# Four pieces of weight decoding move from slots 3 and 4 to slots 20 to 23

## The chip, the cores and the metric

The kernel runs on one core of a Trainium2 chip. The metric is the device time of one execution in microseconds (us), lower is better. Engines: PE is TensorE (matrix products), DVE is VectorE, ACT is ScalarE, POOL is GpSimd, and SP is SyncE, whose queue issues the DMA transfers.

## What is computed

Three stages follow each other. A recurrent state of 40x40 per batch and head walks over 768 steps and gives one vector per step; the 3072 vectors go through a first MLP (320 to 1024, a softmax-gated unit, a layer norm, back to 320) and a second one (320 to 2048, a leaky unit, back to 320). Cut to what matters:

```python
for t in range(S):                                   # S = 768, 4 batches x 8 heads, D = 40
    y[:, :, t] = np.einsum('bhd,bhde->bhe', rt, state)
    Sa = np.einsum('bhde,bhe->bhd', state, at)
    state_decay = state * wt[:, :, None, :] - np.einsum('bhd,bhe->bhde', Sa, bt)
    state = state_decay + np.einsum('bhd,bhe->bhde', vt, kt)
...
h = x @ w_in                                         # first MLP, 3072 x 320 -> 1024
e = np.exp(h - h_max)
solu = h * e / (np.sum(e, axis=-1, keepdims=True) + 1e-09)
ln = (solu - mu) / np.sqrt(var + 1e-06) * g_ln
x = ln @ w_out                                       # 1024 -> 320
...
h = x @ w_in                                         # second MLP, 320 -> 2048
g = np.maximum(h, 0.0) + alpha * np.minimum(h, 0.0)
out = g @ w_out                                      # 2048 -> 320
```

## The kernel before

**Slots.** The recurrence is cut into 24 slots of 32 steps (`slot(g)`, g from 0 to 23). In each slot the state enters as `px` (L430, copied to `XP` by ACT at L433; this document counts a slot from that copy), then `pu` = `XP` times an inverted triangular matrix `LMN` (L443), `pf` (L466), `pst` and the state update `VUS` (L478, L483), `pss` (L501), `py` (L541), and so to the next slot's `px`. Every fourth slot needs a new inverse: its elimination steps (L355 and L359 alternately, some 30 pairs of shrinking or growing width) run on DVE through two slots and end in a transposition, L388; the first `pu` that reads it is that of slot 4, 8, 12 and so on. Scans over the decay (L281, L277) and factors for the key tiles (`kbf`, L303) are DVE's too; `kbf` is loaded by L230, two transfers per two slots.

**The first MLP lags.** In slot g the tokens of step group g-3 go through the first product (`mm1`, L576, from `xt` to `h`) and the softmax (`soft`: L581 row maximum on DVE, L582 exponential on ACT, L583 on DVE, L585 square on ACT, which frees `h`); those of group g-4 are normed (L593), transposed (`tr1`, L615, to `lnh` at L620 and `lnl` at L621) and go through the second product (`mm2`, L629 to L631). `mm1` of the next group needs `h` free. PE's order is written out by hand and is the same in both kernels, instruction for instruction. The other engines are put in order by a scheduler when the program is built, so the change moves rows on them that the diff doesn't show.

**Weight decoding.** The weights arrive in 64-bit floats and are turned to 32 bits on the chip in 51 pieces (11 for the first MLP, 40 for the second). `dec(n)` in `slot` takes the next n pieces off one list, always in the same order. A piece loads `raw` (L681, SP), runs `decode`: L657 and L658 on DVE, L659 and L660 on ACT, L661 and L663 on DVE, L666 on POOL; a piece of the second MLP is then written to DRAM (L717, SP; to `wd` or `od`). The first pieces are 512 wide, the later ones 256. A 256-wide piece has buffers of its own. A **wide** piece borrows the MLP's: `raw` takes the buffer of `lnh` or `P` (alternating) and `wem` that of `lnl`, each of which exists once. Piece 16 (counted from 0) is the last wide one; its `raw` sits in `P`, the buffer that `soft` writes, and is both read and overwritten there, so that `P` is free only when its L717 has left.

**Phase 2.** After slot 23 the second MLP runs; its weights come back from `wd` and `od` through `w2l` (L964, L965), split by ACT (L966) and POOL (L968, L969).

How many pieces a slot takes is set by tables: `ND` for slots 0 to 3, `NL` for slots 20 to 23, `NC` for the others, by g % 4.

## Time and profile before

| | |
|---|---|
| median of 3 runs | 1150.07 us (1148.67 to 1155.81) |
| the profiled execution | 1149.97 us, its span 1148.2 us |
| busy, PE / DVE / ACT / POOL | 976.5 / 790.7 / 519.9 / 496.7 us |
| mean granted clock of PE | 0.896 of full speed |
| slots 3, 4 | 176.2 to 206.6 to 247.4 us |
| slots 6, 7, 8 | 275.7 to 302.8 to 324.6 to 362.5 us |
| slots 20 to 23 | 667.0 to 695.3 to 720.3 to 739.7 us and on |
| second MLP alone | from about 818 us to the end |

No engine is busy all the time in phase 1: the slots are chains that pass from engine to engine. So the question at each place is which wait ends last there. A row of the timeline gives the start, the time, the engine, the line, the operation and in brackets how long the engine stood idle before and who released it.

### The profile page before, as it was taken

To read this page: it belongs to the slowest core of one execution; us is meant where nothing else is said; L and a number is where in the kernel's file an instruction comes from. 1 tells how busy PE (TensorE), PEld (TensorE's weight loads), DVE (VectorE), ACT (ScalarE), POOL (GpSimd) and SP (SyncE) were. 2 spreads that over 40 slices of the span, in tenths; PEclk is the share of its full clock that TensorE was granted. 3 is DMA by queue.
4 is the path that set the end of the run, shared out by engine and by line. 5 is a ranking of instruction groups with operands and counts; after the bars stand their busy time and mean duration, and the time that the engine had idled before them with its cause. 6 is when DMAs were issued, how large, how long until landed. Compare 5 with 4: busy or idle time off the path is not lost.

```text
span 1148.2 us, 37076 instructions
## 1 busy us (share of the span) xinstructions
PE 976.5 (85%) x15913; PEld 810.8 (71%) x15934; DVE 790.7 (69%) x1610; ACT 519.9 (45%) x1198; POOL 496.7 (43%) x546
## 2 busy tenths in 40 slices
PE   6275686688888988798888887989999999999997
PEld 3243454476666767677667666778999988888897
DVE  8899689877997898888978966467444444444433
ACT  3435454376547663765466647656312121212121
POOL 6847454444444443443344425345333333333332
PEclk8687878699888888986888889999999999999999
DMA  5513335344434433442334333354202020201000
GB/s 166 149 49 92 97 113 145 94 110 110 116 104 104 118 94 95 109 128 73 102 94 105 102 111 98 100 169 134 91 1 69 1 69 1 69 1 47 1 23 15
DMA packets 104543, 99.52 MB, mean 87 GB/s; under 512 B 38068, under 2 KB 83764, under 8 KB 104372
## 3 DMA queue, kind: packets, MB, share of 16 engines
q1 hardware_dynamic: 104372, 97.07, 30.5%
q8 instruction: 127, 2.08, 0.8%
q14 instruction: 44, 0.36, 0.1%
HBM read 71.62 MB, written 25.43 MB: 85 GB/s over the span
## 4 chain that ended last, share of the span: by engine, by line
PE 49%; DVE 29%; ACT 6%; issue 6%; POOL 5%; DMA 4%; SPq 0%; DVEq 0%; POOLq 0%; ACTq 0%
PE ph L1016 15%; PE h L576 5%; PE acc L1036 5%; PE acc L1035 5%; PE acc L1034 5%; DVE LMN L359 4%; DVE tmp L355 3%; DMA kbf<-in_kb_fm_dram 3%; DVE VUS L483 2%; DVE H L277 2%; PE pf L466 2%; DVE KBS L509 2%; DVE XS L336 2%; DVE kbf L303 1%; PE pg L326 1%
## 5 line engine op out<-in xcount | busy, mean ns | idle before, releaser
L1023 POOL TENSOR_TENSOR gll<-gt,gh 128x512 fp32r<-128x512 f32 (+1 forms) x112 | 129.0, 1152 | 224.0 <-ACT gh L1022 222.9
L596 DVE TENSOR_SCALAR gt<-ph,al 128x512 f32<-128x512 f32 (+1 forms) x112 | 75.5, 674 | 189.7 <-PE ph L1016 189.6
L1022 ACT CAST gh<-gt 128x512 fp32r<-128x512 f32 (+1 forms) x112 | 62.5, 559 | 254.5 <-DVE gt L597 212.6
L576 PE MATMUL h<-w1h,xt 128*128 128x512 f32 x240 | 106.4, 492 | 15.7 <-ACT h L585 15.7
L312 POOL TENSOR_TENSOR XS<-XS,H 40x512 f32<-40x512 f32 (+1 forms) x48 | 68.5, 1432 | 87.2 <-DVE H L277 50.6
L1035 PE MATMUL acc<-w2l,gh 128*128 128x320 f32 x288 | 89.0, 309 | 0.0
L1034 PE MATMUL acc<-w2h,gh 128*128 128x320 f32 x288 | 89.0, 309 | 0.0
L1036 PE MATMUL acc<-w2h,gll 128*128 128x320 f32 x288 | 88.9, 309 | 0.0
L529 POOL TENSOR_TENSOR YS<-YS,mask 64x512 f32<-64x512 f32 x48 | 64.2, 1337 | 49.0 <-ACT YS L528 44.4
L211 PE MATMUL busy<-busy 128*128 128x512 bf16 x200 | 60.1, 454 | 24.6 <-DVE tmp L355 19.6
L359 DVE TENSOR_TENSOR LMN<-LMN,tmp 128x87 f32<-128x87 f32 (+25 forms) x189 | 75.9, 413 | 2.7
L355 DVE TENSOR_TENSOR tmp<-LMN,LMN 128x87 f32<-128x87 f32 (+25 forms) x189 | 71.9, 392 | 3.4
L597 DVE SCALAR_TENSOR_TENSOR gt<-ph,gt 128x512 f32<-128x512 f32 (+1 forms) x112 | 68.8, 615 | 3.7
L576 PEld LDWEIGHTS h<-w1h,xt 128*128 128x128 f32 x240 | 51.2, 224 | 25.5 <-ACT h L585 17.8
L576 PE MATMUL h<-w1l,xt 128*128 128x512 f32 x144 | 68.8, 478 | 0.0
L629 PE MATMUL po<-wo1h,lnh 128*128 128x320 f32 x192 | 66.9, 348 | 0.5 <-DVE lnl L621 0.5
L630 PE MATMUL po<-wo1l,lnh 128*128 128x320 f32 x192 | 61.5, 320 | 0.0
L631 PE MATMUL po<-wo1h,lnl 128*128 128x320 f32 x192 | 61.5, 320 | 0.0
L1016 PE MATMUL ph<-w1h,w2h 128*128 128x512 f32 x180 | 59.3, 394 | 0.0
L211 PEld LDWEIGHTS <-busy 128*128 128x128 bf16 x221 | 23.0, 112 | 50.9 <-DVE busy L946 19.3
L326 PE MATMUL pg<-XS,kbf 104*32 104x64 f32 x1536 | 39.6, 243 | 21.6 <-DVE kbf L303 10.8
L582 ACT ACTIVATE P<-h,sm 128x1024 f32<-128x1024 f32 x24 | 26.7, 1114 | 63.0 <-DVE sm L581 60.5
(200 smaller groups left out, 2738.6 us busy)
## 6 DMA issues: line engine op xcount, KB each, us to landing
kbf<-in_kb_fm_dram SPq DMA_DIRECT2D x24, 416.0 KB
x2d<-x SPq DMA_DIRECT2D x24, 320.0 KB
xd<-Y SPq DMA_DIRECT2D x24, 256.0 KB
xt<-xd SPq DMA_DIRECT2D x12, 512.0 KB
raw<-in_w_in_dram SPq DMA_DIRECT2D x20, 256.0 KB
wt<-in_w_fm_dram SPq DMA_DIRECT2D x24, 211.7 KB
raw<-in_w_in_dram SPq DMA_DIRECT2D x8, 512.0 KB
raw<-in_w_out_dram SPq DMA_DIRECT2D x16, 256.0 KB
```

The source lines that it names most:

```text
L211: nc.tensor.matmul(st["busy"], lhsT=busy[:, 0:128], rhs=busy, start=True, stop=True)
L312: (nc.vector if w < 2 and e in DA else nc.gpsimd).tensor_tensor(out=o, in0=o, in1=h, op=ALU.mult)
L355: eng.tensor_tensor(out=tv[:, a - rows[0][0]:b - rows[0][0]], in0=M[:, a:b, s:s + 1].to_broadcast(sh), in1=l.unsqueeze(1).to_broadcast(sh) ...
L359: r = eng.tensor_tensor(out=o, in0=o, in1=tv[:, a - rows[0][0]:b - rows[0][0]], op=ALU.add)
L576: nc.tensor.matmul(st["h"][:, ns], lhsT=l, rhs=r, start=j == 0, stop=j == len(ops) - 1)
L596: nc.vector.tensor_scalar(out=tmp, in0=h, scalar1=0.0, scalar2=al, op0=ALU.min, op1=ALU.mult)
L597: nc.vector.scalar_tensor_tensor(out=o, in0=h, scalar=0.0, in1=tmp, op0=ALU.max, op1=ALU.add)
L1016: nc.tensor.matmul(p, lhsT=l, rhs=r, start=j == 0, stop=j == len(ops) - 1)
L1023: nc.gpsimd.tensor_tensor(out=gll, in0=t, in1=f32(gh), op=ALU.subtract)
L1034: nc.tensor.matmul(acc, lhsT=gh[:, cs], rhs=oh, start=f == 0, stop=False)
L1035: nc.tensor.matmul(acc, lhsT=gh[:, cs], rhs=ol, start=False, stop=False)
L1036: nc.tensor.matmul(acc, lhsT=gll[:, cs], rhs=oh, start=False, stop=f == K2 - 1)
```

## The change

The tables move four pieces. Pieces per slot before: 6, 6, 4, 2 in slots 0 to 3, then 2, 3, 1, 0 four times, then 3, 3, 3, 0. After: 6, 6, 4, 0, then 0, 3, 1, 0, then 2, 3, 1, 0 three times, then 4, 4, 4, 1. The order of the pieces stays, so from slot 3 on every slot works on pieces up to four places further back in the list: piece 16, the wide one, is called in slot 5 in place of slot 3.

```diff
-VS, NC, NL = 0, (2, 3, 1, 0), (3, 3, 3, 0)
-ND = (6, 6, 4, 2)
+VS, NC, NL = 0, (2, 3, 1, 0), (4, 4, 4, 1)
+ND = (6, 6, 4, 0)
...
         nd = (ND if g < 4 else NL if g >= NG - 4 else NC)[g % 4]
+        if g == KEND:
+            nd = 0
         invs(0.2)
```

`KEND` is 4. Lines below this place are two higher in the changed kernel (L964 to L969 become L966 to L971).

**DVE in slot 3, the last third of the inverse that slot 4 uses.** L355 and L359 are the elimination steps; `sm` holds the softmax's columns of token group 0. Before, the softmax's L583 stands behind the inverse's end:

```order
L355 TENSOR_TENSOR tmp<-LMN_162,LMN_160 128x87
L359 TENSOR_TENSOR LMN_162<-LMN_162,tmp 128x29x3
L384 SCALAR_TENSOR_TENSOR LMN_162<-LMN_162,LMN_160 128x30 x2
L384 SCALAR_TENSOR_TENSOR LMN_162<-LMN_162,LMN_160 128x31
L388 STREAM_TRANSPOSE LMN_160<-LMN_162 128x32x32
L583 SCALAR_TENSOR_TENSOR P,sm<-h,P 128x1024
L586 TENSOR_SCALAR sm<-sm 128x1
L657 TENSOR_SCALAR em_2620<-raw_2619 128x256
L584 TENSOR_SCALAR sm<-sm 128x1
L587 TENSOR_SCALAR sm<-sm 128x1
```

In the changed kernel it stands earlier, between elimination steps of width 231 and 220; the four operations on `wem` of the wide piece, which stood before the step of width 192, are gone from here:

```order
L359 TENSOR_TENSOR LMN_162<-LMN_162,tmp 128x20x12
L483 TENSOR_TENSOR VUS_163<-pst,VUS_164 40x320
L355 TENSOR_TENSOR tmp<-LMN_162,LMN_160 128x231
L583 SCALAR_TENSOR_TENSOR P,sm<-h,P 128x1024
L359 TENSOR_TENSOR LMN_162<-LMN_162,tmp 128x21x11
L584 TENSOR_SCALAR sm<-sm 128x1
L586 TENSOR_SCALAR sm<-sm 128x1
L355 TENSOR_TENSOR tmp<-LMN_162,LMN_160 128x220
L587 TENSOR_SCALAR sm<-sm 128x1
```

L583 moved from behind L388 to some 25 rows ahead of it; L582 on ACT moves with it, to right behind L528 of the same slot.

**DVE in slot 6, the first half of the inverse that slot 8 uses.** `lnl` is the buffer of the second product's low half, `ptr` the transposed tokens. Before, the two L621 of token group 2 stand at the start of the inverse:

```order
L367 STREAM_TRANSPOSE LMN_162<-LMN_161 128x32x32
L621 TENSOR_TENSOR lnl<-ptr,lnh 128x512
L483 TENSOR_TENSOR VUS_164<-pst,VUS_163 40x320
L384 SCALAR_TENSOR_TENSOR LMN_161<-LMN_162,LMN_161 128x31
L384 SCALAR_TENSOR_TENSOR LMN_161<-LMN_162,LMN_161 128x30 x2
L483 TENSOR_TENSOR VUS_164<-pst,VUS_163 40x320
L355 TENSOR_TENSOR tmp<-LMN_161,LMN_162 128x87
L483 TENSOR_TENSOR VUS_164<-pst,VUS_163 40x320
L359 TENSOR_TENSOR LMN_161<-LMN_161,tmp 128x3x29
L483 TENSOR_TENSOR VUS_164<-pst,VUS_163 40x320
L355 TENSOR_TENSOR tmp<-LMN_161,LMN_162 128x112
L621 TENSOR_TENSOR lnl<-ptr,lnh 128x512
```

In the changed kernel the wide piece comes first, behind the row maximum L581 of the next token group, and L621 follows it:

```order
L581 TENSOR_REDUCE sm<-h 128x1
L657 TENSOR_SCALAR wem<-raw 128x512
L658 TENSOR_SCALAR wem<-raw 128x512
L359 TENSOR_TENSOR LMN_161<-LMN_161,tmp 128x10x22
L355 TENSOR_TENSOR tmp<-LMN_161,LMN_162 128x231
L661 SCALAR_TENSOR_TENSOR wem<-raw,wem 128x512
L663 SCALAR_TENSOR_TENSOR wem<-raw,wem 128x512
L359 TENSOR_TENSOR LMN_161<-LMN_161,tmp 128x11x21
L355 TENSOR_TENSOR tmp<-LMN_161,LMN_162 128x240
L621 TENSOR_TENSOR lnl<-ptr,lnh 128x512 x2
L359 TENSOR_TENSOR LMN_161<-LMN_161,tmp 128x12x20
L355 TENSOR_TENSOR tmp<-LMN_161,LMN_162 128x247
```

The two L621, one at the inverse's first rows and one after its second pair of steps before, now stand together behind step 240, behind the wide piece's `wem`, which holds the `lnl` buffer until its L666 on POOL has read it. Two rows further on moved with them: L545, which waits for `py` and stood ahead of the inverse's first step of width 220, now stands some fourteen steps later, behind the second one of width 255; and in slot 7 the softmax's L583, which stood 22 rows ahead of L388, now stands five rows behind it.

**SP where phase 1 ends, in slot 23 and just behind.** `od_103<-dec` writes decoded pieces, `xd<-Y` and `xt<-xd` move the recurrence's last outputs to the first MLP, `w2l` are the decoded weights that come back. Before:

```order
L717 DMA od_103<-dec 128x256
L965 DMA w2l_11902<-od_101 128x640
L560 DMA xd_79<-Y 32x8x256
L560 DMA xd_79<-Y 8x8x256
L560 DMA xd_79<-Y 32x8x256
L560 DMA xd_79<-Y 8x8x256
L561 DMA xt<-xd_79 128x4x256
L650 DMA x2d_89<-x_11937 640x1x128
L562 DMA xt<-xd_79 128x256
```

In the changed kernel:

```order
L717 DMA od_103<-dec 128x256
L681 DMA raw_11540<-in_w_out_dram 128x512
L560 DMA xd_79<-Y 32x8x256
L560 DMA xd_79<-Y 8x8x256
L717 DMA od_103<-dec 128x256
L681 DMA raw_11751<-in_w_out_dram 128x512
L560 DMA xd_79<-Y 32x8x256
L560 DMA xd_79<-Y 8x8x256
L717 DMA od_103<-dec 128x256
L561 DMA xt<-xd_79 128x4x256
L562 DMA xt<-xd_79 128x256
```

Before, one decoded piece is still to be written here, ahead of the last moves of `Y`; now three are, each behind its own chain of decoding, and two loads of `raw` stand between, all ahead of the `xt` loads.

## Rows read from the trace of the kernel before

**Rows 1.** Page, part 4: the chain that ended last, shares of the span by engine

```profile
PE 49%; DVE 29%; ACT 6%; issue 6%; POOL 5%; DMA 4%; SPq 0%; DVEq 0%; POOLq 0%; ACTq 0%
```

**Rows 2.** Stretches: start:end and length, busy us (x instructions) per engine, clock, DMA

```profile
206.60:247.40 40.80, 26.43 (x644) 21.17 (x645) 35.26 (x75) 23.11 (x52) 17.14 (x19) 0.79 0.36 92
695.30:777.00 81.70, 72.51 (x1439) 61.72 (x1438) 47.30 (x104) 52.03 (x112) 34.24 (x38) 0.98 0.43 125
818.00:1148.20 330.20, 322.43 (x1845) 293.07 (x1843) 131.38 (x198) 66.78 (x123) 115.98 (x98) 0.99 0.10 28
```

**Rows 3.** DVE in slots 3 and 4: start, us, line, operation, [idle before, releaser]

```profile
193.31 1.21 DVE L581 TENSOR_REDUCE sm<-h 128x1 f32<-128x1024 f32 x1
...
199.68 0.42 DVE L657 TENSOR_SCALAR wem<-raw 128x512 int32<-128x512 int32 x1
...
201.63 0.68 DVE L663 SCALAR_TENSOR_TENSOR wem<-raw,wem 128x512 f32<-128x512 uint32 x1
...
206.67 1.30 DVE L355 TENSOR_TENSOR tmp<-LMN,LMN 128x156 f32<-128x156 f32 x1
208.01 0.32 DVE L359 TENSOR_TENSOR LMN<-LMN,tmp 128x156 f32<-128x156 f32 x1
...
212.01 2.01 DVE L388 STREAM_TRANSPOSE LMN<-LMN 128x1024 f32<-128x1024 f32 x1
```

**Rows 4.** ACT in slot 4

```profile
210.03 1.11 ACT L582 ACTIVATE P<-h,sm 128x1024 f32<-128x1024 f32 x1 [2.46 <-DMA od<-raw]
```

**Rows 5.** POOL in slot 4

```profile
206.53 1.26 POOL L666 TENSOR_TENSOR raw<-wem 128x512 f32<-128x512 f32 x1
```

**Rows 6.** SP (the DMA queue's issues) in slots 4 and 5

```profile
207.82 0.35 SPq L717 DMA_DIRECT2D od<-raw  x1
...
251.76 0.63 SPq L650 DMA_DIRECT2D x2d<-x  x1
254.10 0.36 SPq L717 DMA_DIRECT2D wd<-dec  x1
254.83 0.33 SPq L230 DMA_DIRECT2D kbf<-in_kb_fm_dram  x1
```

**Rows 7.** PE in slot 4

```profile
217.10 0.79 PE L576 MATMUL h<-w1h,xt 128*128 128x512 f32 x1 [10.63 <-ACT h L585]
...
221.73 0.39 PE L576 MATMUL h<-w1l,xt 128*128 128x512 f32 x1
222.05 0.79 PE L443 MATMUL pu<-XP,LMN 32*32 32x40 f32 x64
```

**Rows 8.** Chain of waits, first transfers of wide pieces: start, us, what

```profile
155.80 4.06 DMA raw<-in_w_in_dram
```

**Rows 9.** DVE in slot 6

```profile
283.66 0.69 DVE L621 TENSOR_TENSOR lnl<-ptr,lnh 128x512 fp32r<-128x512 f32 x1
...
294.68 1.21 DVE L581 TENSOR_REDUCE sm<-h 128x1 f32<-128x1024 f32 x1
```

**Rows 10.** PE in slots 6 to 8

```profile
285.39 0.38 PE L615 MATMUL ptr<-ident,P 128*128 128x128 f32 x2
...
288.67 0.31 PE L629 MATMUL po<-wo1h,lnh 128*128 128x320 f32 x1
...
297.63 0.80 PE L430 MATMUL px<-VUS,XS 104*32 104x40 f32 x64 [2.45 <-DVE Yt L545]
...
304.99 1.29 PE L443 MATMUL pu<-XP,LMN 32*32 32x40 f32 x64
...
329.47 0.78 PE L443 MATMUL pu<-XP,LMN 32*32 32x40 f32 x64 [4.02 <-DVE LMN L388]
```

**Rows 11.** Groups by line and shape: DVE work of 256-wide pieces (count, busy, mean ns)

```profile
L658 DVE TENSOR_SCALAR em<-raw 128x256 int32<-128x256 int32 x36 | 18.0, 500 | 0.0
...
L663 DVE SCALAR_TENSOR_TENSOR em<-raw,em 128x256 f32<-128x256 uint32 x36 | 17.3, 480 | 0.4 <-ACT em L660 0.3
L657 DVE TENSOR_SCALAR em<-raw 128x256 int32<-128x256 int32 x36 | 16.8, 466 | 5.3 <-DMA raw<-in_w_in_dram 2.6 <-DMA raw<-in_w_out_dram 1.7 <-POOL Y L550 0.7
...
L661 DVE SCALAR_TENSOR_TENSOR em<-raw,em 128x256 int32<-128x256 int32 x36 | 16.2, 450 | 5.6 <-ACT em L659 4.8
```

**Rows 12.** DVE in slot 20

```profile
709.46 1.80 DVE L663 SCALAR_TENSOR_TENSOR em<-raw,em 128x256 f32<-128x256 uint32 x1
```

**Rows 13.** SP where phase 1 ends

```profile
763.74 0.38 SPq L561 DMA_DIRECT2D xt<-xd  x1
```

**Rows 14.** PE where phase 1 ends

```profile
777.75 0.48 PE L576 MATMUL h<-w1h,xt 128*128 128x512 f32 x1
```

## Prediction

> **What bounds the kernel now.** I read the page's chain first: PE holds 49% of it, DVE 29% [rows 1]. Then I cut the span into stretches. From about 818 us on, only the second MLP runs: PE is busy 322.43 of 330.20 us [rows 2]. The change touches nothing there but the last loads of its weights, so this stretch is fixed and the time is decided in the slots before it. There, DVE is the fullest engine in slot 4 (35.26 of 40.80 us) but far from full in slots 21 to 23 and just behind (47.30 of 81.70 us) [rows 2]. So decoding costs more in slot 4 than at the end, if DVE's busy time alone decided. The timelines say that waits decide as much, and where they sit.
>
> **The wait that the change removes (slots 3 and 4).** The row maximum of token group 0 ends on DVE at 194.52 [rows 3]. The exponential that needs it starts only at 210.03, and its releaser is the transfer `od<-raw` [rows 4]: the wide piece sits in buffer `P` from its load to its store. Its DVE work runs from 199.68 to 202.31 [rows 3], POOL multiplies from 206.53 to 207.79 [rows 5], SP issues the store at 207.82 [rows 6], and 2.2 us later `P` is free. Behind it wait L583, L585, then `mm1` on PE, which stood idle for 10.63 us until 217.10, and behind `mm1`, in PE's fixed order, `pu` of slot 4 at 222.05 [rows 7]. In the changed kernel L582 and L583 are in slot 3, before the inverse's last third, so `h` is free before `px(4)`, and `mm1` runs in PE's idle time. What `pu` then waits for is the inverse: L388 ends at 214.02 [rows 3]. DVE loses there the wide piece's four operations and gains L583, about even, since DVE waits for `py` in between anyway. One step of 128x156 took 1.30 us beside POOL's L666, against 0.32 us for its neighbour of the same width [rows 3, 5]; without the wide piece that is 0.98 us less. So L388 ends at about 213.0 and `pu` moves from 222.05 to 213.0: **9.0 us earlier at this point**.
>
> How much is left at the start of slot 6? DVE has only 40.80 - 35.26 = 5.54 us of idle time in slot 4 [rows 2], so a PE that runs ahead soon waits for DVE. But pieces 18 and 19 leave slot 4 too. A 256-wide piece costs DVE 500 + 480 + 466 + 450 ns = 1.90 us [rows 11]. Two are 3.80 us, and 5.54 + 3.80 = 9.34 us would allow the 9.0. In slot 5 the second `kbf` load is issued at 254.83, behind the store of a decoded piece at 254.10, and the chain of slot 5 goes through it; the store of the first MLP's output, at 251.76 for 0.63 us, is the next one in front [rows 6]. Without the decoded piece the load goes out at 252.39 less the shift of the slot itself. Bounds for the gain at slot 6: 3.8 us, if only the DVE work counts, and 9.0 us, if all of `pu`'s shift lives on. I take **8.0**, near the upper end, because DVE, `pu` and the load all move by about this much.
>
> **The wait that it makes (slots 6 to 8).** Piece 16 now runs in slot 6. Its `raw` needs `P`, which the transposition of token group 2 reads until PE's L615 at 285.39 [rows 10]; a wide load then takes some 4.06 us [rows 8], so it lands at 290 at the earliest. But its DVE rows stand behind L581, at 294.68 to 295.89 [rows 9]. The four of them took 2.63 us in slot 3 [rows 3], so they end at about 298.5; L666 takes 1.26 us [rows 5], 299.8; then both L621, 0.69 us each [rows 9]: the first product that reads `lnl` can start at about 300.5 to 301. Before, L621 ran at 283.66 [rows 9] and `mm2` of group 2 began at 288.67 [rows 10]. PE thus waits about 12 us in times of the kernel before, with `py` and `px(7)` queued behind. `px(7)` stood at 297.63, with 2.45 us of waiting for DVE [rows 10]; it comes some 9 to 11.5 us later, and `pu(7)`, at 304.99, about 9.3 us later. After that there is slack: DVE goes on with the inverse for slot 8 in the meantime, and before the change PE waited 4.02 us for L388 at `pu(8)`, 329.47 [rows 10]. 9.3 - 4.0 = 5.3. The inverse itself loses almost nothing, as more of its steps now stand ahead of L545, which waits for `py`. But L583 of the next token group now stands behind L388 in DVE's order, so the `mm1` that waits for it in slot 7 can't run ahead of the inverse's end. I take a **loss of 5.0 us**; bounds 1.0 (the inverse alone decides `pu(8)`) and 11.5 (all of `px(7)`'s shift stays).
>
> **The slots between.** From slot 8 to 19 the counts per slot are the same; the pieces are other ones of the same width. I put this at 0.
>
> **The end (slots 20 to 23).** Four pieces more: 4 x 1.90 = 7.60 us of DVE [rows 11], in slots where DVE is idle for 42% of the time [rows 2]. Bounds: 0, if all of it falls into idle time, and 7.6. What speaks for more than 0: the pieces follow each other through one set of buffers (load, DVE, ACT, DVE, POOL, store), and in SP's order the `xt` loads of the last tokens stand behind two more of them. L561 was issued at 763.74 [rows 13] and its tokens were used at 777.75 [rows 14], so some 14 us of delay are hidden before that load decides. DVE is busy 58% of the time there, and 0.58 x 7.6 = 4.4 us would push something else back, if that lay on the chain each time. I take **3.0 us**, two thirds of that, by my judgement.
>
> At this place a rule bears on the price. One L663 in slot 20 took 1.80 us [rows 12] against 0.48 in the mean [rows 11], and the step of 128x156 took 1.30 beside L666 [rows 3, 5]. The Trainium skill, GPSIMD Engine Reference, section Key points, says that GpSimd shares its SBUF interfaces with VectorE and that they get in each other's way when a VectorE instruction has two SBUF inputs or runs in a two-port mode; the traces agree with these two numbers. By that rule each of the four added L666 holds up one DVE instruction by 0.98 us, and the end costs 3.0 + 4 x 0.98 = 6.9 in place of 3.0.
>
> **The sum.** 1149.97 (the profiled execution, span 1148.2; 0.10 under the median) - 8.0 + 5.0 + 3.0 + 0 = 1149.97, so **1150 us**: no change. With all bounds low, 1149.97 - 9.0 + 1.0 + 0 = 1142; with all high, 1149.97 - 3.8 + 11.5 + 7.6 = 1165.
>
> **Rivals.**
> - *The new wait is absorbed.* If PE catches up by `pu(8)`, because the inverse ends first and last there anyway, the loss is 1.0 and the end costs 2: 1149.97 - 8 + 1 + 2 = 1145 us. For it: the 4.02 us that PE waited for L388 [rows 10]. Against it: L583 behind L388, and 9.3 is more than 4.02.
> - *The new wait is not absorbed (slower).* Place: `mm2` of group 2 in slot 6, held by `lnl`. Price: all 11.5 us of `px(7)`'s shift, with the end at 3: 1149.97 - 8 + 11.5 + 3 = 1156.5, and 1161 with the end at its bound of 7.6. It decides as soon as it costs more than the 5.0 us that the removed wait leaves over after the end's 3.0. For it: PE's order is fixed, so `py`, `px(7)` and `pu(7)` all queue behind, and DVE is nearly full in these slots. Against it: the 4.02 us.
> - *The gain dies in slot 4.* If DVE or the `kbf` load holds slot 5 where it was, only 3.8 remain: 1149.97 - 3.8 + 5 + 3 = 1154 us. For it: 5.54 us of DVE idle time are less than 9.0. Against it: 3.8 us of DVE work leave as well.
> - *POOL and DVE collide at the end*, the mechanism of 0.98 us per piece: 1149.97 - 8 + 5 + 6.9 = 1154 us. For it: the 1.80 us [rows 12]. Against it: most pieces there ran at their mean.
>
> **How the numbers follow.** Chances: forecast (1147 to 1153) 0.40, absorbed 0.22, not absorbed 0.23, gain dies 0.10, collision 0.05. The range must reach to the absorbed case with the gain at its bound of 9.0 (1144) and a little slack of mine in the slots between, and upward nearly to the dear end of the second rival: 1141 to 1160; some 0.2 lies outside, more of it above. The forecast's own range is 1147 to 1153. One per cent, 11.5 us, is about what a measurement of this kernel can tell from no change. Faster by over 1% (under 1138.6) needs more than every gain that I found: 0.06. Slower by over 1% (over 1161.6) is the second rival at its dear end, or with another cost: 0.14. Within: 0.80.
>
> **What would show it.** In the profile of the changed kernel: L576 in slot 4 without its 10.63 us of waiting for L585, and `pu(4)` released by L388, some 9 us earlier; slot 6 starting 8 us earlier; L629 in slot 6 released by L621 after some 12 us; `pu(8)` about 3 us earlier than 329.47; the `xt` load at the end some 10 us closer to its use. I am wrong if the wide piece's load comes much later or earlier than L615's end, if PE does not wait at L629, or if the slots from 8 on, where I expect nothing, drift by more than a few us.

## The result: 1164.28 us, 1.25% slower

The changed kernel takes 1164.28 us in the median of 6 runs (1160.15 to 1167.18); the kernel before, beside it, 1149.37 (1142.04 to 1156.53, 6 runs). The ratio is 1.0125, 95% interval 1.0093 to 1.0156. The forecast was 1150, its range ended at 1160. The profiled executions differ by 15.6 us (spans 1148.2 and 1163.8), which is what is taken apart here.

The starts of the slots (the copy to `XP`) show where, in us:

| stretch | before | after | difference | forecast |
|---|---|---|---|---|
| start of slot 2 to slot 4 | 55.9 | 56.0 | +0.2 | 0 |
| slots 4 and 5 | 69.1 | 66.8 | -2.3 | -8 |
| slots 6 and 7 | 48.9 | 61.8 | +12.9 | +5 |
| slots 8 to 19 | 342.4 | 336.1 | -6.3 | 0 |
| slot 20 to the end | 481.2 | 492.9 | +11.7 | +3 |

Up to slot 2 the two agree within 0.6 us. In this pair of traces all four terms came out as other sizes, and the three that the forecast had sized were all too friendly. How far one trace can be trusted, and what the terms cost in timed runs, follows with the experiments.

The chain on the page (shares of the span by engine) has moved from PE and DVE to DMA, POOL and ACT, against [rows 1]:

```profile
PE 45%; DVE 27%; ACT 7%; DMA 7%; POOL 7%; issue 5%; SPq 1%; POOLq 0%; DVEq 0%; ACTq 0%
```

**Slot 4: as predicted.** PE, and DVE and POOL beside it, in the changed kernel; the bracket is the idle time before and who ended it. `mm1` no longer waits for L585, where it stood idle for 10.63 us before [rows 7]; `pu` waits for L388 and starts at 212.94. The working had said 213.0. That the two agree to 0.1 us is luck: slot 4 began 0.4 us earlier than before, and L388, counted from there, ended 0.8 us earlier and not 0.98 (6.60 us after the start of the slot in place of 7.40). The cause of it is as worked out: before, two steps of the inverse in this slot took 1.26 to 1.30 us, one beside POOL's L666 and one beside its L550 (208.91 to 210.17); now only the one beside L550 does.

```profile
206.01 0.80 PE L576 MATMUL h<-w1h,xt 128*128 128x512 f32 x1
206.63 1.26 POOL L550 TENSOR_TENSOR Y<-Yt,Y 104x512 fp32r<-104x512 f32 x1
206.64 1.44 DVE L359 TENSOR_TENSOR LMN<-LMN,tmp 128x156 f32<-128x156 f32 x1
...
210.78 2.00 DVE L388 STREAM_TRANSPOSE LMN<-LMN 128x1024 f32<-128x1024 f32 x1
...
212.94 0.78 PE L443 MATMUL pu<-XP,LMN 32*32 32x40 f32 x64 [3.06 <-DVE LMN L388]
```

**Slot 5: the gain is cut down by ScalarE's order.** PE finishes with `px(5)` at 238.7; `px` moved as far as one could ask, but its copy to `XP`, with which slot 5 starts, stands on ACT behind eight copies to `KBS` (L405, L406) and a cast. It ran at 243.82, 3.6 us earlier than before.

```profile
237.84 0.89 PE L430 MATMUL px<-VUS,XS 104*32 104x40 f32 x64
```

```profile
240.44 0.29 ACT L405 COPY KBS<-pt 64x160 f32<-64x160 f32 x1
...
243.24 0.29 ACT L406 COPY KBS<-pt 64x160 f32<-64x160 f32 x1
...
243.82 0.43 ACT L433 COPY XP<-px 128x320 f32<-128x320 f32 x1
```

**Slot 6: the wait, as long as predicted, and dearer.** DVE reaches L581 at 291.02, then the wide piece; POOL's L666 frees `lnl` at 296.27, and L621 follows.

```profile
291.02 1.21 DVE L581 TENSOR_REDUCE sm<-h 128x1 f32<-128x1024 f32 x1
292.16 0.41 DVE L657 TENSOR_SCALAR wem<-raw 128x512 int32<-128x512 int32 x1
...
294.15 0.68 DVE L663 SCALAR_TENSOR_TENSOR wem<-raw,wem 128x512 f32<-128x512 uint32 x1
...
296.45 1.28 DVE L621 TENSOR_TENSOR lnl<-ptr,lnh 128x512 fp32r<-128x512 f32 x2
```

```profile
294.97 1.30 POOL L666 TENSOR_TENSOR raw<-wem 128x512 f32<-128x512 f32 x1 [7.54 <-DVE wem L663]
```

PE stands at L629 for 11.47 us (predicted: about 12). Then `px(7)`, `pu(7)`, `px(8)` and `pu(8)`, to compare with [rows 10]:

```profile
297.19 0.63 PE L629 MATMUL po<-wo1h,lnh 128*128 128x320 f32 x1 [11.47 <-DVE lnl L621]
...
306.23 0.80 PE L430 MATMUL px<-VUS,XS 104*32 104x40 f32 x64
...
309.89 0.79 PE L443 MATMUL pu<-XP,LMN 32*32 32x40 f32 x64
...
327.20 0.80 PE L430 MATMUL px<-VUS,XS 104*32 104x40 f32 x64
...
337.42 0.79 PE L443 MATMUL pu<-XP,LMN 32*32 32x40 f32 x64
```

`pu(7)` is 4.9 us later than before; slot 6 had started 2.8 us earlier, so the wait cost 7.7 us up to there, a little less than the 9.3 of the working. But `pu(8)` is 7.95 us later, at 337.42 in place of 329.47, where the forecast had it 3 us earlier. Between the two, slot 8 lost what it was meant to win back: `px(8)` is done at 328, its copy to `XP` runs at 334.76, 6.8 us after `px(8)` ended, where it was 2.1 us before (322.46 to 324.59). On DVE, L583 stands behind L388 (transposition, then the softmax):

```profile
325.39 2.16 DVE L388 STREAM_TRANSPOSE LMN<-LMN 128x1024 f32<-128x1024 f32 x1
...
329.09 1.23 DVE L583 SCALAR_TENSOR_TENSOR P<-h,P 128x1024 f32<-128x1024 f32 x1
```

and on ACT, L585 waits for it, L593 waits for L585's chain, and the copy to `XP` stands behind both:

```profile
330.56 1.12 ACT L585 ACTIVATE h<-P,sm 128x1024 f32<-128x1024 f32 x1 [1.97 <-DVE sm L584]
...
333.62 1.24 ACT L593 ACTIVATE P<-P,sm 128x1024 f32<-128x1024 f32 x1 [0.59 <-POOL sm L590]
334.76 0.40 ACT L433 COPY XP<-px 128x320 f32<-128x320 f32 x1
```

There is a second cost, which no term had; it is a part of the 7.7 us. In windows of slots 6 and 7 (first row) and of the eighteen products behind the wait (second row), the clock column, third from the right, reads 0.82 and 0.50 in the changed kernel:

```profile
272.90:334.80 61.90, 44.97 (x1021) 36.85 (x1022) 56.43 (x122) 33.27 (x81) 19.73 (x26) 0.82 0.34 94
297.20:302.30 5.10, 5.10 (x19) 4.77 (x19) 4.93 (x13) 2.02 (x4) 0.00 (x0) 0.50 0.65 179
```

and 0.93 and 1.00 in the kernel before:

```profile
275.70:324.60 48.90, 43.47 (x1028) 35.34 (x1027) 45.07 (x101) 32.23 (x81) 20.77 (x28) 0.93 0.39 102
288.70:291.30 2.60, 2.60 (x19) 2.50 (x17) 2.50 (x4) 0.00 (x0) 1.81 (x2) 1.00 0.84 270
```

After 11.47 us without work, PE ran these products at half its full clock, 1.2 instead of 2.4 GHz: the first eighteen took 5.1 us, where they took 2.6 to 2.7.

**The end.** SP in slot 22, the kernel before in the first row, then the changed kernel: the store of a decoded piece is issued at 743.32, having waited 11.3 us for the piece's work on DVE, ACT and POOL; behind it a load of `raw`, and only then the `xt` load, at 744.23. The one like it was issued at 730.57 in the kernel before; slot 22 itself had begun 5.6 us earlier there (720.28 and 725.89), so 8 of the 13.7 us came within the slot.

```profile
730.57 0.39 SPq L561 DMA_DIRECT2D xt<-xd  x1
```

```profile
743.32 0.34 SPq L717 DMA_DIRECT2D wd<-dec  x1
743.76 0.38 SPq L681 DMA_DIRECT2D raw<-in_w_in_dram  x1
744.23 1.00 SPq L561 DMA_DIRECT2D xt<-xd  x1
```

PE waits for that load:

```profile
749.41 0.50 PE L576 MATMUL h<-w1h,xt 128*128 128x512 f32 x1 [1.73 <-DMA xt<-xd]
```

and DVE stands still three times behind a load of `raw` in slots 22 and 23, for 4.3 us in all (from slot 20 on for 5.4 us, in the kernel before for 3.8):

```profile
746.73 1.00 DVE L657 TENSOR_SCALAR em<-raw 128x256 int32<-128x256 int32 x1 [1.59 <-DMA raw<-in_w_in_dram]
...
755.91 0.29 DVE L657 TENSOR_SCALAR em<-raw 128x256 int32<-128x256 int32 x1 [0.82 <-DMA raw<-in_w_out_dram]
...
760.82 1.22 DVE L657 TENSOR_SCALAR em<-raw 128x256 int32<-128x256 int32 x1 [1.86 <-DMA raw<-in_w_out_dram]
```

The forecast had looked at this queue for the last `xt` load, with 14 us to spare [rows 13, 14]. The one that was caught was the load before it. The whole loss lies ahead of the last product of the first MLP: from its start to the end of the kernel both traces have 334 us, as the forecast had it for that stretch.

### The profile page after: what moved, and what is told of

Its sections match the earlier page's. It is cut to its first block, busy times and chain, and to the rows that moved or that the text cites. A ratio compares the mean times of both kernels' runs of the same rounds, so it can differ in the third digit from the quotient of the medians.

```text
span 1163.8 us, 37092 instructions
## 1 busy us (share of the span) xinstructions
PE 982.9 (84%) x15934; PEld 814.1 (70%) x15934; DVE 790.7 (68%) x1610; ACT 521.4 (45%) x1198; POOL 499.1 (43%) x546
## 4 chain that ended last, share of the span: by engine, by line
PE 45%; DVE 27%; ACT 7%; DMA 7%; POOL 7%; issue 5%; SPq 1%; POOLq 0%; DVEq 0%; ACTq 0%
PE ph L1018 15%; PE acc L1038 5%; PE acc L1036 5%; PE acc L1037 5%; PE h L576 4%; DMA kbf<-in_kb_fm_dram 4%; DVE tmp L355 3%; DVE LMN L359 3%; DVE VUS L483 2%; DMA raw<-in_w_out_dram 2%; DVE KBS L509 2%; DVE kbf L303 2%; DVE sm L581 1%; DVE H L277 1%; PE pf L466 1%
## 5 line engine op out<-in xcount | busy, mean ns | idle before, releaser
L1025 POOL TENSOR_TENSOR gll<-gt,gh 128x512 fp32r<-128x512 f32 (+1 forms) x112 | 128.6, 1149 | 222.4 <-ACT gh L1024 221.3
L576 PE MATMUL h<-w1h,xt 128*128 128x512 f32 x240 | 109.5, 506 | 6.2 <-ACT h L585 4.5
L312 POOL TENSOR_TENSOR XS<-XS,H 40x512 f32<-40x512 f32 (+1 forms) x48 | 66.1, 1380 | 81.3 <-DVE H L277 46.0
L211 PE MATMUL busy<-busy 128*128 128x512 bf16 x221 | 64.4, 445 | 17.3 <-DVE busy L948 16.0
L629 PE MATMUL po<-wo1h,lnh 128*128 128x320 f32 x192 | 67.9, 353 | 11.5 <-DVE lnl L621 11.5
L359 DVE TENSOR_TENSOR LMN<-LMN,tmp 128x87 f32<-128x87 f32 (+25 forms) x189 | 73.4, 400 | 2.7
L355 DVE TENSOR_TENSOR tmp<-LMN,LMN 128x87 f32<-128x87 f32 (+25 forms) x189 | 72.3, 394 | 3.6
L576 PEld LDWEIGHTS h<-w1h,xt 128*128 128x128 f32 x240 | 53.6, 234 | 16.5 <-ACT h L585 5.9
L582 ACT ACTIVATE P<-h,sm 128x1024 f32<-128x1024 f32 x24 | 26.8, 1115 | 81.4 <-DVE sm L581 73.3
L666 POOL TENSOR_TENSOR dec<-em 128x256 f32<-128x256 f32 x36 | 30.7, 852 | 64.1 <-DVE em L663 35.3
L541 PEld LDWEIGHTS py<-YS,KBS 128*40 128x40 f32 (+1 forms) x1536 | 36.8, 135 | 28.5 <-issue 12.2
```

Source lines behind the costliest of these rows:

```text
L312: (nc.vector if w < 2 and e in DA else nc.gpsimd).tensor_tensor(out=o, in0=o, in1=h, op=ALU.mult)
L355: eng.tensor_tensor(out=tv[:, a - rows[0][0]:b - rows[0][0]], in0=M[:, a:b, s:s + 1].to_broadcast(sh), in1=l.unsqueeze(1).to_broadcast(sh) ...
L359: r = eng.tensor_tensor(out=o, in0=o, in1=tv[:, a - rows[0][0]:b - rows[0][0]], op=ALU.add)
L576: nc.tensor.matmul(st["h"][:, ns], lhsT=l, rhs=r, start=j == 0, stop=j == len(ops) - 1)
L629: nc.tensor.matmul(po, lhsT=lh[:, k], rhs=wo1h[:, k], start=k == 0, stop=False)
L1025: nc.gpsimd.tensor_tensor(out=gll, in0=t, in1=f32(gh), op=ALU.subtract)
```

## The experiments

Sixteen kernels were timed, six to twelve runs each, beside the kernel before on the same chip. In e1 to e9, e12 and e16 the tables are replaced by one tuple of the number of pieces per slot, read by `nd = NDS[g]`, as here; what some of them change beside it stands with them. e10, e11, e13 and e15 are the changed kernel with the edit shown, and e14 is the kernel before with the edit shown:

```diff
-VS, NC, NL = 0, (2, 3, 1, 0), (4, 4, 4, 1)
-ND = (6, 6, 4, 0)
+VS = 0
+NDS = (6, 6, 4, 0, 0, 3, 1, 0, 2, 3, 1, 0, 2, 3, 1, 0, 2, 3, 1, 0, 4, 4, 4, 1)   # this one: the changed kernel
```

Results, with the stretches of each profiled execution (us). The ratios are estimates of their own against the kernel before, timed beside each group (medians 1148.95 to 1150.29 us), and not quotients of the medians in this table. A profiled execution can lie some us off the median of its kernel (e13: 1167.9, its slowest; e1: 1162.67). Kernels with the same instruction order differ by up to some 3 us in slots 2 to 7 and at the end (before and e4: 55.9 and 53.1 in slots 2 and 3), and by more in slots 8 to 19: five with the order of the kernel before on DVE, ACT and POOL there took 338.0 to 348.4 (before, e2, e6, e9, e14), four with the order of the changed kernel 335.3 to 341.5 (after, e8, e13, e15).

| kernel | median | ratio (95%) | slots 2-3 | 4-5 | 6-7 | 8-19 | 20-end |
|---|---|---|---|---|---|---|---|
| before | 1149.37 | 1 | 55.9 | 69.1 | 48.9 | 342.4 | 481.2 |
| after | 1164.28 | 1.0125 (1.0093-1.0156) | 56.0 | 66.8 | 61.8 | 336.1 | 492.9 |
| e1 spread | 1166.68 | 1.0153 (1.0117-1.0189) | 56.3 | 66.4 | 61.7 | 341.8 | 484.8 |
| e2 wide early | 1151.15 | 1.0005 (0.9977-1.0034) | 56.3 | 64.7 | 49.0 | 343.3 | 488.9 |
| e3 wide early, spread | 1165.09 | 1.0148 (1.0112-1.0185) | 56.1 | 65.5 | 49.5 | 358.4 | 484.5 |
| e4 tail only | 1154.42 | 1.0035 (1.001-1.0059) | 53.1 | 70.0 | 48.7 | 344.5 | 487.0 |
| e5 wide cut | 1155.2 | 1.0052 (1.0021-1.0083) | 54.6 | 65.4 | 48.6 | 345.5 | 487.9 |
| e6 wide early only | 1148.61 | 0.9997 (0.9967-1.0026) | 56.6 | 66.8 | 48.8 | 348.4 | 483.0 |
| e7 all early | 1160.9 | 1.0124 (1.0078-1.017) | 64.7 | 64.0 | 48.5 | 347.1 | 483.3 |
| e8 tail front | 1164.69 | 1.013 (1.0091-1.0168) | 55.7 | 65.7 | 61.4 | 336.3 | 495.2 |
| e9 four dropped | 1148.8 | 0.9984 (0.9956-1.0011) | 55.1 | 67.0 | 49.5 | 338.0 | 483.8 |
| e10 P alone | 1163.45 | 1.012 (1.007-1.017) | 55.5 | 63.4 | 56.9 | 343.8 | 490.9 |
| e11 XP by DVE | 1165.01 | 1.0122 (1.0073-1.0172) | 55.7 | 62.7 | 59.4 | 344.8 | 494.4 |
| e12 before, cut | 1151.57 | 1.0025 (0.9994-1.0055) | 57.1 | 67.3 | 48.1 | 344.5 | 481.6 |
| e13 half the loads | 1159.8 | 1.0094 (1.006-1.0128) | 56.1 | 67.1 | 61.7 | 341.5 | 488.8 |
| e14 plain early | 1147.04 | 0.997 (0.9939-1.0001) | 53.1 | 66.5 | 48.1 | 344.5 | 482.0 |
| e15 plain late | 1160.69 | 1.0102 (1.0064-1.0141) | 55.8 | 64.3 | 61.2 | 335.3 | 489.9 |
| e16 cut, plain late | 1152.45 | 1.0028 (0.9998-1.0058) | 54.8 | 67.3 | 50.4 | 340.4 | 487.8 |

### What makes the loss in slots 6 and 7

The theory is that the borrowed buffers make it; the rival, that the work does. Two kernels take the borrowing out: e2 has the wide piece in slot 2, e5 cuts it in two of 256.

```diff
+NDS = (6, 6, 5, 0, 0, 3, 1, 0, 2, 3, 1, 0, 2, 3, 1, 0, 2, 3, 1, 0, 4, 4, 4, 0)   # e2_wide_early
```

> Counts 6, 6, 5, 0, 0, 3, 1, 0 and then as changed, with 4, 4, 4, 0 at the end: the wide piece runs in slot 2, where the first MLP has not begun, and nothing runs in slots 3 and 4. Theory (the wide piece's hold on lnl and P makes the loss in slot 6): no wait of mm2 for L621 in slot 6, the 11 to 13 us between slot 6 and slot 8 gone, three added pieces at the end cost three quarters of 11.5 us: 1148 to 1153 us. Rival (slot 6 is full with any piece, of whatever width): the loss stays, 1160 us or more.

```diff
+NDS = (6, 6, 4, 0, 0, 4, 1, 0, 2, 3, 1, 0, 2, 3, 1, 0, 2, 3, 1, 0, 4, 4, 4, 1)   # e5_wide_cut
...
-                t += [(wo[:, :, b + a:b + z], od[j // 2][:, a:z]) for a, z in cuts(4 * DM, j < JW)]
+                cs = cuts(4 * DM, j < JW)
+                if j < JW:
+                    cs = [cs[0], (512, 768), (768, 1024)] + cs[2:]
+                t += [(wo[:, :, b + a:b + z], od[j // 2][:, a:z]) for a, z in cs]
```

> The changed kernel with piece 16 cut into two pieces of 256, both in slots 5 and 6 (counts 0, 4, 1, 0 in slots 4 to 7), so that it borrows neither P nor lnl; the end stays 4, 4, 4, 1. Theory (the loss in slots 6 and 7 comes from the borrowed buffers, not from the work): slot 8 starts within 3 us of the kernel before in place of 10 us later, and the whole takes 1164.3 - 11 = about 1153 us (1149 to 1157). Rival (the work of that piece in slots 5 and 6 is what costs): 1160 us or more.

Both came out as the theory said: 1151.15 and 1155.2 us, and slots 6 and 7 take 49.0 and 48.6 us, as before, in place of 61.8. (Slot 8 of e5 was expected within 3 us of the kernel before and began 7.0 us earlier, at 317.57.) PE in e5, the first product of `mm2`, then `px(7)`, `pu(7)` and `pu(8)`: no wait for L621, and `pu(8)` waits for L388 again, 4.77 us.

```profile
281.50 0.31 PE L629 MATMUL po<-wo1h,lnh 128*128 128x320 f32 x1
...
290.11 0.80 PE L430 MATMUL px<-VUS,XS 104*32 104x40 f32 x64 [1.29 <-DVE Yt L545]
...
297.60 1.29 PE L443 MATMUL pu<-XP,LMN 32*32 32x40 f32 x64
...
323.12 1.24 PE L443 MATMUL pu<-XP,LMN 32*32 32x40 f32 x64 [4.77 <-DVE LMN L388]
```

So the buffers are the cause of the 12.9 us, and e5 puts their price at the end of the kernel at 1.0125 - 1.0052 = 0.73%, 8.4 us (with both intervals, some 3 to 13). A second pair, e15 and e16 further down, differs in the same edit: 1.0102 - 1.0028 = 0.74%, 8.5 us. Both differences include what else the scheduler changed with the edit, from slot 20 on for instance (492.9 us in the changed kernel, 487.9 in e5).

Which buffer? e10 loads the wide piece into `P` as before but decodes it in two halves through the small buffers, so that `lnl` is free (the piece is the ninth wide one).

```diff
+PIECE = 9
...
+            st["words"] = st.get("words", 0) + 1
+            if st["words"] == PIECE:
+                nc.sync.dma_start(out=raw.rearrange("p (k n) -> p k n", k=src.shape[1]), in_=src.bitcast(U32))
+                for q in range(2):
+                    em = m1.tile([128, 2, 256], I32, name="em2")
+                    decode(raw[:, q * 512:q * 512 + 512], em[:, 0], em[:, 1], raw[:, q * 512:q * 512 + 256].bitcast(F32))
+                return raw.rearrange("p (q z) -> p q z", q=2)[:, :, 0:256].bitcast(F32)
```

> The changed kernel with the wide piece loaded as one block into P as before, but decoded in two halves through the small buffers, so that it holds P and not lnl. Theory (lnl, for which mm2 and all of PE behind it wait, makes the loss): no wait of 11 us at L629 in slot 6, slot 8 starts 5 us earlier to 1 us later than before, 1151 to 1157 us. Rival (P, for which the softmax of slot 6 waits, makes it): slot 8 still 5 to 10 us late, 1160 us or more.

Neither side was right. `mm2` no longer waits, and `px(7)` is early; but the softmax waits for `P` (the piece's store leaves at 293.32, the exponential runs at 296.23), and `mm1` behind it for 8.15 us, so that `pu(7)` comes at 304.50, where it came at 297.60 in e5:

```profile
300.90 0.80 PE L577 MATMUL h<-w1h,xt 128*128 128x512 f32 x1 [8.15 <-ACT h L586]
...
304.50 0.94 PE L444 MATMUL pu<-XP,LMN 32*32 32x40 f32 x64
```

Slots 6 and 7 take 56.9 us: 8 of the 13 us are there with `P` alone. The whole kernel took 1163.45 us, no less than the changed one: at the end of the kernel the hold on `P` alone costs what both cost. A hold on `lnl` alone was not tried. Why the 5 us that e10 wins in slots 6 and 7 are gone by the end is not settled; its slots 8 to 19 took 343.8 us, those of the changed kernel 336.1.

### What taking the pieces out of slots 3 and 4 is worth

Three kernels take the wait of slot 4 away and add nothing at the end: e6 (the wide piece to slot 2), e12 (cut in two, in slots 3 and 4) and e14 (plain copies in the place of all four pieces, the most there is to win). e9 leaves the four out too, with the copies issued at the start.

```diff
+NDS = (6, 6, 5, 1, 2, 3, 1, 0, 2, 3, 1, 0, 2, 3, 1, 0, 2, 3, 1, 0, 3, 3, 3, 0)   # e6_wide_early_only
+NDS = (6, 6, 4, 2, 3, 3, 1, 0, 2, 3, 1, 0, 2, 3, 1, 0, 2, 3, 1, 0, 3, 3, 3, 0)   # e12_before_cut, with e5's cut
```

> The kernel before with only the wide piece moved, from slot 3 to slot 2: counts 6, 6, 5, 1 and all else as before. Theory (the wait of slot 4 for P is worth what reached slot 5 in the changed kernel, 3 us): mm1 in slot 4 without its wait of 10.6 us, pu(4) 6 to 9 us earlier, 1 to 4 us of that left at slot 6 and at the end: 1145 to 1149 us. Rival (the prediction's step: all of it lives on): 1141 to 1143 us. Second rival (slot 2 is as full, the gain is paid there): 1149 to 1152 us.

> The kernel before with piece 16 cut into two of 256 and one piece more in slot 4 (counts 6, 6, 4, 2, then 3, 3, 1, 0, then as before): nothing moves to the end, and the softmax of slot 3 doesn't wait for P. Theory (that wait is worth 3 to 4 us at slot 6): 1145 to 1148 us. Rival (the piece more in slot 4 takes it back): 1149 to 1152 us.

```diff
-        return [lambda a=a: chunk(*a) for a in t]
+        def plain(src, dst):
+            nc.sync.dma_start(out=dst, in_=v.rearrange("b h (u s) d -> (b h u) (s d)", u=4)[:, 0:dst.shape[1]])
+
+        return [lambda a=a, f=plain if 5 <= i < 9 else chunk: f(*a) for i, a in enumerate(t)]   # e14_plain_early
```

> The kernel before with pieces 16 to 19 replaced, in their places in slots 3 and 4, by plain copies of other data from DRAM to DRAM, so that part of the weights is wrong: no decoding and no hold on P and lnl there, nothing added at the end. It measures the most that taking the four pieces out of slots 3 and 4 can give. Theory (2 to 4 us at slot 6, as read from the runs so far): 1144 to 1148 us. The prediction's step (8 us): 1140 to 1143 us. Rival (nothing of it lives on): 1148 to 1151 us.

```diff
+NDS = (6, 6, 4, 0, 0, 3, 1, 0, 2, 3, 1, 0, 2, 3, 1, 0, 2, 3, 1, 0, 3, 3, 3, 0)   # e9_four_dropped
...
-        return [lambda a=a: chunk(*a) for a in t]
+        for src, dst in t[5:9]:
+            nc.sync.dma_start(out=dst, in_=v.rearrange("b h (u s) d -> (b h u) (s d)", u=4)[:, 0:dst.shape[1]])
+        return [lambda a=a: chunk(*a) for a in t[:5] + t[9:]]
```

> Pieces 16 to 19 are left out: plain copies of other data, issued before the slots, stand in for them, so that part of the second MLP's weights is wrong; counts 6, 6, 4, 0, 0, 3, 1, 0, then as before with 3, 3, 3, 0 at the end, and the pieces of slots 20 to 23 are the same as in the kernel before. Nothing borrows P or lnl in slots 3 to 6. Theory (the end's four pieces cost 6 to 10 us): the start of slot 8 as in the kernel with the cut piece, some 7 us earlier than before, and the end as before: 1143 to 1149 us. Rival (the end's pieces cost at most 3 us, as predicted): 1151 us or more.

e6 and e12 gave 0.9997 and 1.0025: no change that can be told (e6's time lies in its theory's range, e12's in its rival's). e14, with none of the four pieces left, gave 0.997, that is 3.4 us, at most 7, and its interval just reaches no change. In e14, too, `pu(4)` waits for nothing but the inverse; it stands 12 us earlier than before, of which 3.5 are slot 4's earlier start:

```profile
209.81 0.83 PE L443 MATMUL pu<-XP,LMN 32*32 32x40 f32 x64 [4.12 <-DVE LMN L388]
```

and slots 4 and 5 are 2.6 us shorter. (In the four kernels with the changed kernel's order they take 64.3 to 67.1 us, mean 66.0, in the two with the order before 69.1 and 70.0.) e9 gave 0.9984; its slot 0 started at 48.68 where the other kernels' started between 41.4 and 44.7, which the copies at the start explain, so it says the same as e14 within its error, less directly.

Is it ACT's order in slot 5 that keeps the gain small? e11 lets DVE write `XP` there.

```diff
-        nc.scalar.copy(out=XP.rearrange("p (s d) -> p s d", d=D), in_=px)
+        if g == 5:
+            nc.vector.tensor_copy(out=XP.rearrange("p (s d) -> p s d", d=D), in_=px)
+        else:
+            nc.scalar.copy(out=XP.rearrange("p (s d) -> p s d", d=D), in_=px)
```

> The changed kernel with one copy moved: XP of slot 5 is written by VectorE in place of ScalarE, so that it stands behind no KBS copies. Theory (ScalarE's order ate 4 us of the gain at slot 5): XP of slot 5 some 7 us earlier than in the kernel before in place of 3.6 us, slot 6 some 5 to 7 us earlier, and 3 us less in all: 1159 to 1163 us. Rival (the next wait, for the kbf load or for DVE, eats it in slot 5 anyway): slot 6 as in the changed kernel, 1163 to 1167 us.

At the place, yes: `XP` of slot 5 is written at 237.15, 10.3 us earlier than in the kernel before, and slots 4 and 5 take 62.7 us, where the four kernels with the changed kernel's order take 66.0 in the mean.

```profile
237.15 0.49 DVE L434 COPY XP<-px 128x320 f32<-128x320 f32 x1
```

At the end, no: 1165.01 us, as the changed kernel. The rival had this time, but not the place: slot 6 starts 5.4 us ahead of the changed kernel (267.62 and 272.98) and slot 8 7.7 us ahead (327.01 and 334.76). Slot 20 starts 1.0 us behind it: slots 8 to 19 took 344.8 us in place of 336.1. e11 is not alone in this. Over the fifteen kernels with the same counts in slots 8 to 19, a slot 8 that starts 1 us earlier goes with a slot 20 that starts only about 0.5 us earlier (an estimate, a straight line through the starts, correlation 0.7). Why these slots give back half of a lead was not tried.

### What the end costs

```diff
+NDS = (6, 6, 4, 2, 2, 3, 1, 0, 2, 3, 1, 0, 2, 3, 1, 0, 2, 0, 0, 0, 4, 4, 4, 1)   # e4_tail_only
+NDS = (6, 6, 4, 0, 0, 3, 1, 0, 2, 3, 1, 0, 2, 3, 1, 0, 2, 3, 1, 0, 5, 5, 3, 0)   # e8_tail_front
```

> The kernel before with four pieces moved from slots 17 and 18 to the end: counts as before up to slot 15, then 2, 0, 0, 0 and 4, 4, 4, 1; slots 3 and 4 and the wide piece are as before. Theory (the added pieces at the end are a loss by themselves): from the start of slot 20 to the end some 11 us longer than before; slots 16 to 19 some 2 to 6 us shorter; 1153 to 1159 us. Rival (the end is only late because the slots before were late): the stretch from slot 20 as long as before, 1143 to 1148 us.

> The changed kernel with the end as 5, 5, 3, 0 in place of 4, 4, 4, 1: as many pieces in slots 20 to 23, none of them behind slot 22. Theory (what costs at the end are the last pieces, whose loads and stores stand in front of the moves that the first MLP waits for): 4 to 8 us less than the changed kernel, 1156 to 1160 us. Rival (each piece costs what it costs wherever it stands in these slots): 1162 to 1167 us.

e4 has nothing of the change but the end, and is 0.35% slower, 4 us, though slots 17 and 18 lost four pieces. So the end is a loss by itself, of 1.2 to 6.8 us by the interval. Its time lies in its expected range, its parts don't: the stretch from slot 20 on is 5.8 us longer, where 11 were expected, and slots 16 to 19 are no shorter (114.0 and 113.5 us). Over all kernels, the stretch from slot 20 on takes 481.2 to 484.8 us where the counts are 3, 3, 3, 0 (eight kernels: before, e1, e3, e6, e7, e9, e12, e14) and 487.0 to 494.4 where they are 4, 4, 4, 1 with all pieces decoded (after, e4, e5, e10, e11): means of 483.0 and 490.6, **7.6 us** apart. But the five are of two kinds. In the changed kernel, e10 and e11 both `xt` loads of slot 22 stand on SP behind a store that is held, and PE's `mm1` waits for them (1.73, 2.00 and 2.32 us): 492.9, 490.9 and 494.4. In e4 and e5 the first of them goes out ahead of that store, and PE waits for neither: 487.0 and 487.9. SP in e4:

```profile
730.07 0.38 SPq L561 DMA_DIRECT2D xt<-xd  x1
738.66 0.32 SPq L717 DMA_DIRECT2D wd<-dec  x1
739.07 0.38 SPq L562 DMA_DIRECT2D xt<-xd  x1
```

So the pieces by themselves cost 4.4 us here, as e4's runs say, and the kind of order that the changed kernel got costs some 5 more (492.7 in the mean against 487.5). e8 shows that an earlier place within these slots helps nothing: 495.2 and 1164.69 us; its `mm1` waits 2.39 us for the load.

For the cause, e13 leaves out every second load there, e15 and e16 the decoding of the last four pieces, with the `plain` of e14 (for `36 <= i < 40` in e15; in e16, which has e5's cut and counts as well, for `37 <= i < 41`). e13's edit:

```diff
+            again = st["slot"] >= NG - 4 and "again" in st
+            raw = st.pop("again") if again else m1.tile([128, 512], U32, name="raw2")
+            if st["slot"] >= NG - 4 and not again:
+                st["again"] = raw
...
+        if n > 256 or not again:
+            nc.sync.dma_start(out=raw.rearrange("p (k n) -> p k n", k=src.shape[1]), in_=src.bitcast(U32))
```

> The changed kernel, but in slots 20 to 23 every second piece decodes the block that the piece before it loaded: 6 loads are left out, and with them half of the last weights are wrong; the work of all engines stays. Theory (the pieces at the end wait for each other's loads, some 3 us each): the stretch from slot 20 to the end is 5 to 8 us shorter, 1156 to 1160 us. Rival (the work on DVE, ACT and POOL costs, not the loads): 1162 to 1166 us.

> The changed kernel with its last four pieces replaced by plain copies, so that part of the weights is wrong; slots 3 to 8 as in the changed kernel, with the wide piece in slot 6. The difference to the changed kernel is the price of the end. Theory (7 us): 1155 to 1159 us. The prediction's step (3 us): 1160 to 1163 us.

> Both losses taken out: the wide piece cut in two as in the earlier run, and the last four pieces replaced by plain copies, so that part of the weights is wrong. What is left against the kernel before is the gain alone. Theory (2 to 4 us and 7 us for the end): 1145 to 1149 us. The prediction's step (gain of 8 us): 1140 to 1143 us.

e13 took 1159.8 us, e15 1160.69: 4.5 and 3.6 us less than the changed kernel, within their errors, and from slot 20 on they still take 488.8 and 489.9. e16 took 1152.45, 2.8 less than e5. By the words of its expectation e15 came out on the prediction's side, 1160 to 1163: the decoding of the last four pieces costs 0.23% between it and the changed kernel and 0.24% between e16 and e5, under 3 us. e16 shows no gain at all, where 1145 to 1149 was expected. So neither the loads nor the last four pieces' work is the whole of the end. What e15, e16 and the changed kernel share is that eight pieces, in place of six, stand in slots 20 and 21, and that SP's queue has a held store in slot 22: ahead of both `xt` loads in the changed kernel and e15, where PE's `mm1` waits 2.59 us and the chain of waits goes through that load, ahead of the second alone in e16, where it doesn't wait. In e13 the stores ahead of these loads are held for 3 us at the most and PE doesn't wait for the loads, so its shorter stretch doesn't speak for the loads of `raw` alone. The queue was not tried by itself: DVE and ACT have other orders too in the kernels that are compared.

### Other places for the four pieces

```diff
+NDS = (6, 6, 4, 0, 0, 3, 1, 1, 2, 3, 1, 1, 2, 3, 1, 1, 2, 3, 1, 1, 3, 3, 3, 0)   # e1_spread
+NDS = (6, 6, 5, 0, 0, 3, 1, 1, 2, 3, 1, 1, 2, 3, 1, 1, 2, 3, 1, 0, 3, 3, 3, 0)   # e3_wide_early_spread
+NDS = (7, 7, 6, 0, 0, 3, 1, 0, 2, 3, 1, 0, 2, 3, 1, 0, 2, 3, 1, 0, 3, 3, 3, 0)   # e7_all_early
```

> The changed kernel, but the four pieces go one each to slots 7, 11, 15 and 19; slots 20 to 23 take 3, 3, 3, 0 as before. Theory (two losses: the wide piece holds lnl in slot 6, and the four added pieces at the end wait for each other's loads): slots 3 to 8 as in the changed kernel (slot 8 some 10 us later than before), the stretch from slot 20 to the end as long as before, which takes 11.5 us off, and up to 1.9 us for each of the four slots: 1153 to 1158 us. Rival (the end costs nothing, all is lost in slot 6): 1162 us or more.

> Both at once: counts 6, 6, 5, 0, 0, 3, 1, 1, then 2, 3, 1, 1 twice, 2, 3, 1, 0, and 3, 3, 3, 0 at the end, so three pieces go to slots 7, 11 and 15. Theory of the two losses: neither is there, the gain of slots 3 and 4 is left (3 us of it reach slot 5 in the changed kernel), up to 1.9 us for each of three slots: 1143 to 1150 us, at or under the kernel before. Rival (the slots between can't hide a piece): 1152 us or more.

> All four pieces earlier in place of later: counts 7, 7, 6, 0, 0, 3, 1, 0 and from slot 8 on as before with 3, 3, 3, 0 at the end. Theory (what slots 3 and 4 gain is 3 to 5 us, and neither of the two losses is there): 1144 to 1148 us, if slots 0 to 2 hide their extra pieces. Rival (slots 0 to 2 wait for decoding themselves): up to 1.9 to 3 us per piece back, 1150 to 1156 us.

All three were dearer than expected. e1 does win the end back (484.8), but its slots 8 to 19 take 341.8 us in place of 336.1, and the whole is no shorter (its profiled execution lies 4 us under its median). e3 has neither the wait of slot 6 nor the dear end, and still takes 1165.09: its slots 8 to 19, which had 342.4 us in the kernel before, take 358.4. It has three pieces of 256 more around them (slots 7, 11 and 15), but so has e1, at 341.8; so the pieces alone don't account for the 16 us, and their cause was not tried further. e7 pays 9 us in slots 2 and 3. No kernel here is faster than the kernel before beyond its error, so none was taken further.

## Why the prediction was wrong

The mechanisms stood where the prediction had put them, with their signs; their sizes were wrong, and all to the same side. By its own terms, from timed runs: the gain is 3.4 us (e14; 0 to 7) in place of 8.0; the wait costs 8.4 and 8.5 (changed kernel less e5, e15 less e16; each some 3 to 13) in place of 5.0; the end costs 4.0 (e4; 1.2 to 6.8), or 7.6 by the means of the stretches, in place of 3.0. 1149.4 - 3.4 + 8.4 + 4.0 = 1158.4, or 1162 with 7.6, where 1164.3 was measured. The sum can't be closed better than that: the terms have errors of 3 to 5 us each, and the 8.4 holds 5 us from slot 20 on, by the profiled executions, that the 7.6 counts too. Of the three sizes only the 8.0 lies outside the interval of the runs made for it; the other two are read from the traces.

- **The wait that is removed.** Right up to `pu(4)`, to 0.1 us by luck. The step that failed is "how much is left at the start of slot 6", 8.0 us, where 2.8 were left. It asked DVE and the `kbf` load and not ACT, whose fixed order holds the copy to `XP` of slot 5. And e14 and e11 show that even what is left at slot 6 reaches the end only in part: e11 began slot 8 7.7 us ahead of the changed kernel and slot 20 behind it.
- **The wait that is made.** 11.47 us at L629 against about 12 predicted, and `pu(7)` as worked out within 2 us. The step that failed is the subtraction 9.3 - 4.0 = 5.3: from the start of slot 6, `pu(8)` came 10.7 us later than before (64.4 us in place of 53.7). It took the 4.02 us for which PE waited for L388 [rows 10] as slack in which the loss would vanish. The working itself named the reason against it, that L583 stands behind L388, and followed it to `mm1` only; by way of L585 and L593 the copy to `XP` of slot 8 also stood behind it on ACT. Slack before one wait is no slack when the engine that releases another moves along. The half clock after the wait was not in the sum either.
- **The slots between.** 0 predicted, -6.3 in the trace. The four kernels with the changed kernel's order there take 337.3 us in the mean, the five with the order before 343.3, so most of it is more than the chance of one trace. Part of it is won back in slot 8 itself (4.2 us). Since the scheduler orders DVE, ACT and POOL anew for these slots, and one order alone varied by 6 to 10 us between kernels, the reason for the rest stays open.
- **The end.** 3.0 predicted, 11.7 in this trace. e4's runs, 4.0 us, don't exclude the 3.0. The step that failed is the look at SP's order: it asked for the last `xt` load and found 14 us to spare, while the loads of slot 22 stood behind a held store. Where they do, the stretch is some 5 us longer than with as many pieces and the first load ahead of the store.
- **The rivals.** The second one, the wait not absorbed, had the sign and the place: 1156.5 to 1161 us at a chance of 0.23. The collision of POOL and DVE, with its 6.9 us for the end, did not come at that size: the mean of DVE's four operations on a piece from slot 20 on rose from 1.94 to 2.23 us by the trace's groups, 0.29 us a piece where it asked for 0.98, on 13 pieces 3.8 us of DVE time at the most. The row that it rested on [rows 12] lies in slot 21, not 20, and ran beside POOL's L969 (709.17 to 710.97), a row of the second MLP's weights, not beside an L666.
- **The range.** "All bounds high" gave 1165, which would have held it; the range was cut to 1160 since the three high ends were taken to be independent. In this trace all three came out high together, each by an engine's or a queue's fixed order behind a wait.

## What to carry to other kernels

A piece of work that borrows another stage's buffer costs by when it holds the buffer, not by its length: 2 us of VectorE time in slot 6 stopped TensorE for 11.5 us. When a wait is followed to its end, follow it through every engine that executes in order, the copying one too: an idle time that PE shows is only slack if what ends it does not move along. And lightly loaded slots near the end are not free, when each piece sends two transfers through the queue that also carries the next stage's input: a store that waits for computed data holds every load behind it, here for 11.3 us.

## What was unexpected of the hardware

After 11.47 us of idle time TensorE's next eighteen products ran at a granted clock of 0.50 (1.2 GHz) and took 5.1 us in place of 2.6 to 2.7; over slots 6 and 7 the mean clock fell from 0.93 to 0.82. And an execution is less repeatable here than its instruction order suggests: the kernel before ranged from 1142.04 to 1156.53 us in six runs, and the stretch from slot 8 to 19 took 338.0 to 348.4 us in five kernels (before, e2, e6, e9, e14) that have the same order on DVE, ACT and POOL there.
